# Values ahead of the first attention step, more staging tiles for the last tokens, earlier value transfers: one change to a two-branch attention kernel

## Chip, cores and metric

The kernel runs on one core of a Trainium2 chip. The metric is the device time of one execution in microseconds (us), lower is better. Every figure below is of executions in the undisturbed ("fast") state; the runs of one kernel lie within 0.1% to 0.7% of each other.

## The reference, cut to what matters

The result is a gated sum of two branches over the same 2048 x 576 input. Branch A is recurrent: 64 segments of 32 tokens, each with 8 memory tokens that the segment before it produced. Branch B is plain softmax attention with 32 heads of 18 columns.

```python
g = sigmoid((x * gate_w).sum(-1))
# A, 32 heads of 128:
for s in range(64):
    h = concat([mem, x[32*s : 32*s+32]])          # 8 + 32 tokens
    q, k, v = h @ Wq, h @ Wk, h @ Wv              # 576 -> 4096 each
    o = softmax(mask(q k^T * scale)) v @ Wo
    mem, out[s] = o[:8], o[8:]                    # mem goes to segment s + 1
# B, 32 heads of 18:
b = softmax(q k^T * scale) v @ wo                 # all 2048 tokens
return g * a + (1 - g) * b
```

Only the memory makes A serial. The q, k and v of tokens do not depend on it, so the kernel computes those of the **last 8 tokens** of each segment ahead of time, for 16 segments together. Branch B is cut into 512 **attention steps** (two groups of matmuls and one Exp of 128x2048 on ScalarE), which fill the gaps that A's chain leaves.

## The kernel before

It has three stages. The **prologue** transposes x, projects Q, K and V of branch B in blocks, stores them in DRAM in a layout by head, loads A's weights (14.2 MB), and does the first of four last-token stages (24 blocks). The **segments** run A, with B's steps and the other last-token stages in between. The **tail** folds the last segments' leftovers and projects the output of B in 16 row blocks.

```python
def load_weights(w, src):                       # six pieces each for wv, wq, wk
    for c in range(NF):
        yield nc.gpsimd.dma_start(out=w[0][:, c, :], in_=...)
    ...
def in_turn(dma):                               # a piece waits for the one before the last
    if len(ready) > 1: add_dependency(dma, ready[-2])
    ready.append(dma)

def last_tokens(q, share, k=None):
    store = nc.sync if share else nc.gpsimd
    xlb = fil.tile([P, NF + 2, P], BF16, name="xlb", bufs=1)
    nc.sync.dma_start(out=xlb..., in_=xld[q])   # the tokens of 16 segments
    for b in range(HD // 512):                  # 8 blocks of V
        ...matmuls into pv...
        vl = fil.tile([P, 512], BF16, name="vl")        # pool fil: two tiles
        copy_out(vl, pv, share); store.dma_start(out=vld[...], in_=vl)
    for w, dstd in ((wq, qld), (wk, kld)):      # 8 + 8 blocks of Q and K
        for b in range(H // 4):
            ...matmuls into pv...
            vl = fil.tile([P, 512], BF16, name="vl")
            copy_out(vl as (s h t), pv as (h s t), share)
            store.dma_start(out=dstd[q]...[:, :, 4*b*LO:4*(b+1)*LO], in_=vl)  # runs of 64 bytes

def project_vb(hf, kb, share):                  # one value block of B, one half of the heads
    vt = vts[kb % 4]                            # four tiles, zero-filled at the start
    ...matmuls into pv...
    copy_out(vt[:, :, 0:DhB], pv, share)
    nc.sync.dma_start(out=vgd[...], in_=vt)
...                                             # prologue: x, blocks 0, 4, 5, first half of the values
for blk in FIRST: store_qk(blk, (0,))
for w, src in ((wv, A_Wv), (wq, A_Wq), (wk, A_Wk)):
    for d in load_weights(w, src): in_turn(d)
...
load_first()                                    # first K, V and Q chunks of B
for blk in FIRST: store_qk(blk, range(1, GB))
for blk in (1, 6, 2, 7): ...project_qk, attention steps between, store_qk...
for kb in range(NKB): project_vb(1, kb, 0); between(0.7)
for blk in (3, 8): ...
```

The softmax here doesn't subtract the row's maximum and nothing guards it: scores larger than these inputs give would overflow.

## Time and profile before

| | before |
|---|---|
| median of the first three runs | 1713.55 us (1712.34 to 1716.27) |
| profiled run (span of the core) | 1708.60 us (1706.9) |
| TensorE, ScalarE, VectorE busy | 88%, 67%, 56% of the span |
| mean granted TensorE clock | 0.967 |
| attention steps done ahead of the segments | 35 of 512 |

In profile rows, PE is TensorE, PEld its weight loads, DVE VectorE, ACT ScalarE, POOL GpSimd and SP SyncE; L823 is a line of the kernel, and `a<-b` means that a is written from b. Of the tiles, kch, vch and qch are chunks of B's K, V and Q, stg stages a Q/K block on its way to DRAM (qtd, ktd), vt stages values of B (to vgd; the five new ones are called xn), vl stages last tokens (tm in the changed kernel's first stage; in the segments tm is a copy of A's new q, k or v), and v_sb holds the values of one segment of A.

The profile gives, for each engine, rows of work with the idle time ahead of them in brackets and what ended that idle time. TensorE is the busiest engine, so its brackets are where time can be had. The prediction shows the large ones. The waits of TensorE summed over the segments are a second view; its columns are engine and line, releaser, us in total, times, longest. First one line of segments 1 to 62, then one of the last-token stage ahead of the segments (155 to 240 us):

```profile
PE pso L823 <- DMA v_sb<-tm: 11.8, 11, 2.3
```

```profile
PE pv L319 <- DVE vl L293: 15.8, 13, 2.5
```

The reader sees two causes that the change addresses: value transfers inside the segments (v_sb<-tm), and staging tiles of the last tokens that are not free yet (vl: 13 waits, none long). A third, the load of the last tokens themselves (xlb), is among the prediction's rows.

### The profile page before, as it was taken

How to read it: one execution, taken by the hardware profiler on the slowest of the kernel's cores; microseconds unless marked ns; L12 is line 12 of the kernel's file. 1: busy time of each engine (PE TensorE's matmuls, PEld its weight loads, DVE VectorE, ACT ScalarE, POOL GpSimd, SP SyncE). 2: the span in 40 equal slices, each digit the busy share in tenths (PEclk: the TensorE clock that was granted, in tenths of full speed). 3: DMA queues.
4: the chain of work that ended last, by engine and by line, in shares of the span. 5: the costliest groups of instructions: out<-in, count | busy, mean ns of one | idle time of the engine just before them, and what ended most of it. 6: DMA issues, size and time to landing. Idle time of an engine off the chain costs nothing. (4 is left out here: it accounts for less than half of the span.)

```text
span 1706.9 us, 57602 instructions
## 1 busy us (share of the span) xinstructions
PE 1494.8 (88%) x25082; PEld 789.3 (46%) x25082; DVE 963.4 (56%) x2360; ACT 1138.6 (67%) x976; POOL 364.6 (21%) x716
## 2 busy tenths in 40 slices
PE   6476669989999899999999999999999989899986
PEld 3232434445555444454555444555554444444444
DVE  2133245666666566656666656666666656565654
ACT  2154335767777676766776767777777787887873
POOL 5211111122222112131313121322221212120221
PEclk9788879999999999999999999999999999999998
DMA  7875431212221111121212111121211111111133
GB/s 191 277 266 185 106 63 33 58 35 46 50 51 45 43 37 52 44 48 35 59 38 56 42 43 47 46 47 36 58 42 48 33 46 32 45 32 31 30 103 103
DMA packets 127464, 114.38 MB, mean 67 GB/s; under 512 B 62531, under 2 KB 115011, under 8 KB 125619
## 3 DMA queue, kind: packets, MB, share of 16 engines
q1 hardware_dynamic: 106395, 59.03, 13.0%
q0 software_dynamic: 19872, 49.38, 10.9%
q8 instruction: 196, 3.21, 0.8%
q10 hardware_dynamic: 944, 2.29, 0.4%
q14 instruction: 57, 0.47, 0.1%
HBM read 60.94 MB, written 36.10 MB: 57 GB/s over the span
## 5 line engine op out<-in xcount | busy, mean ns | idle before, releaser
L257 ACT ACTIVATE etb<-sb 128x2048 bf16<-128x2048 f32 x512 | 959.5, 1874 | 420.2 <-PE sb L238 420.2
L752 DVE CAST tm<-pvv 128x512 bf16<-128x512 f32 x384 | 264.1, 688 | 170.5 <-PE pvv L740 169.1
L740 PEld LDWEIGHTS <-ht 128*32 128x32 bf16 x7680 | 187.0, 97 | 184.3 <-DVE ht L876 12.6
L238 PE MATMUL sb<-qch,kch 32*128 32x512 bf16 x2048 | 204.8, 389 | 55.6 <-ACT etb L257 36.9
L222 PE MATMUL ob<-etb,vch 128*32 128x512 bf16 x2048 | 206.8, 394 | 5.4 <-DVE tq L159 5.1
L835 DVE CAST ot<-pso 128x320 bf16<-128x320 f32 x256 | 120.3, 487 | 124.3 <-PE pso L823 120.5
L629 PE MATMUL acc<-wo,ot 128*32 128x384 bf16 (+1 forms) x4096 | 158.9, 291 | 5.4 <-DVE ot L835 3.6
L740 PE MATMUL pvv<-wq_m,ht 128*32 128x512 bf16 x2048 | 135.9, 386 | 12.6 <-DVE ht L876 7.1
L740 PE MATMUL pvv<-wk_m,ht 128*32 128x512 bf16 x2048 | 134.4, 383 | 0.0
L740 PE MATMUL pvv<-wv_m,ht 128*32 128x512 bf16 x2048 | 134.1, 382 | 0.0
L238 PEld LDWEIGHTS <-kch 32*128 32x128 bf16 x2048 | 61.7, 91 | 146.5 <-issue 111.4
L685 POOL DMA_DIRECT2D a_dram<-rl x192 | 95.9, 534 | 140.3 <-DVE rl L681 136.5
L629 PEld LDWEIGHTS <-ot 128*32 128x32 bf16 x4096 | 104.6, 97 | 45.8 <-DVE ot L835 11.6
L842 POOL COPY otl<-ot 128x256 bf16<-128x256 bf16 x64 | 27.1, 424 | 392.6 <-DVE ot L835 358.9
L222 PEld LDWEIGHTS <-vch 128*32 128x32 bf16 x2048 | 52.7, 93 | 123.7 <-issue 117.3
L293 DVE CAST vl<-pv 128x512 bf16<-128x512 f32 x96 | 65.9, 686 | 73.7 <-DMA qld<-vl 18.6
L823 PE MATMUL pso<-et,v_sb 64*128 64x40 bf16 x2048 | 82.0, 179 | 22.7 <-DMA v_sb<-tm 11.8
L811 ACT ACTIVATE lt<-pss 128x320 f32<-128x320 f32 x128 | 55.9, 437 | 68.0 <-PE pss L807 58.0
L823 PEld LDWEIGHTS <-v_sb 64*128 64x128 bf16 x2048 | 62.9, 93 | 72.5 <-issue 49.0
L767 PE MATMUL pt<-ident,tm 128*128 128x128 bf16 x1024 | 95.7, 221 | 0.8 <-DVE tm L752 0.8
L640 DVE CAST hl<-acc 128x384 bf16<-128x384 f32 (+1 forms) x128 | 57.7, 451 | 56.2 <-PE acc L629 55.9
L775 DVE COPY kt<-pt 128x512 bf16<-128x512 bf16 x128 | 53.8, 420 | 63.0 <-PE pt L767 63.0
(136 smaller groups left out, 1886.9 us busy)
## 6 DMA issues: line engine op xcount, KB each, us to landing
v_sb<-tm SPq DMA_DIRECT2D x512, 32.0 KB
wo<-in_A_Wo_dram POOLq DMA_DIRECT2D x4, 1152.0 KB, 8.1
vgd<-vt SPq DMA_DIRECT2D x32, 128.0 KB
wv_m<-in_A_Wv_dram POOLq DMA_DIRECT2D x4, 1024.0 KB, 8.1
wq_m<-in_A_Wq_dram POOLq DMA_DIRECT2D x4, 1024.0 KB, 8.2
wk_m<-in_A_Wk_dram POOLq DMA_DIRECT2D x4, 1024.0 KB, 9.1
v_sb<-vld SPq DMA_DIRECT2D x128, 32.0 KB
xl<-qld SPq DMA_DIRECT2D x64, 64.0 KB
```

The costliest lines, as they stand in the source:

```text
L222: nc.tensor.matmul(ob[32 * j:32 * j + 32, :], lhsT=vc[:, o + 32 * j:o + 32 * j + 32], rhs=et4[:, j, :], start=(kb == 0), stop=(kb == NKB - 1),
L238: nc.tensor.matmul(sb[:, j, :], lhsT=kc[32 * j:32 * j + 32, o:o + P], rhs=qch[gq][32 * j:32 * j + 32, :], start=True, stop=True, tile_posi ...
L257: nc.scalar.activation(out=before[:, :, :], in_=sb[:, :, :], func=ACT.Exp, scale=scale_b)
L293: nc.vector.tensor_copy(out=out, in_=in_)
L629: nc.tensor.matmul(acc[32 * j:32 * j + 32, 0:d1 - d0], lhsT=o[:, h, 0:CT], rhs=wo[:, h, d0:d1], start=(b == 0 and i == 0), stop=(b == 1 an ...
L640: nc.vector.tensor_copy(out=hl[:, 0, d0:d1], in_=acc[:, 0:d1 - d0])
L685: nc.gpsimd.dma_start(out=rows4[m, seg - LO:seg, i * n:(i + 1) * n], in_=rl[32 * i + m * LO:32 * i + (m + 1) * LO, :],)
L740: nc.tensor.matmul(pv[32 * j:32 * j + 32, :], lhsT=ht[:, cc, :], rhs=rw, start=(c == 0), stop=(c == NF), tile_position=(0, 32 * j),)
L752: nc.vector.tensor_copy(out=sbt[x][:, :], in_=ps[x][:, :])
L767: nc.tensor.transpose(out=pt[:, which, :, :, :].rearrange("p j (u i) t -> p j u i t", i=4)[:, :, :, i, :], in_=sbt[x][:, i * Dh:(i + 1) * Dh],
L823: nc.tensor.matmul(pso[:, i * L:(i + 1) * L], lhsT=v_sb[64 * jj:64 * jj + 64, b * 1024 + i * Dh:b * 1024 + (i + 1) * Dh], rhs=et[64 * jj:6 ...
L835: nc.vector.tensor_copy(out=ot[:, j * HG:(j + 1) * HG, :].rearrange("p h t -> p (h t)"), in_=ps["o", b, jj][:, 0:W8],)
```

## The change

Its intent is to take waits for transfers off TensorE's path at both edges and in the segments:

- The first K, V and Q chunks of B are loaded ahead of A's weights; the weights wait for them.
- All second-half values are projected ahead of every other block and step, into nine tiles instead of four; the five new ones lie on the tiles of x and are zero-filled on GpSimd.
- The first last-token stage gets four staging tiles instead of two. Its rows go to DRAM as whole kilobytes, and the 64-byte runs are on the side that reads them in the segments. Twelve of 14 copies of zero rows (the "pads") move from the prologue into the first segments.
- xlb is loaded one stage ahead; the q and k of the last tokens one segment ahead.
- The value transfer of a segment (`v0`, `v1` in its order) is issued right at its copy (`cV0`, `cV1`).
- In the tail, the leftovers go ahead of all but the first of the 16 row blocks, part of their stores goes to SyncE, and B's last divisions move.

```diff
+    load_first()
+    ready.extend([first_loads[-1]] * 2)
+    for d in pieces:                                  # A's weights
+        in_turn(d)
...
-    for blk in (1, 6, 2, 7):  ...project_qk, between, store_qk...
+    for i in range(5):
+        vt = pw.tile([P, Dm], BF16, name="xn", bufs=5)[:, 0:HV * 32]...
+        nc.gpsimd.memset(vt, 0.0)
+        nc.gpsimd.memset(vt[:, :, DhB:DhB + 1], 1.0)
+        vts.append(vt)
     for kb in range(NKB):
-        project_vb(1, kb, 0)
-        between(0.7)
-    for blk in (3, 8):
+        project_vb(1, kb, 3)
+    for blk in (1, 6, 2, 7, 3, 8):
...
+        stage = (lambda: seg2.tile([P, 512], BF16, name="tm", bufs=4)) if share else (
+            lambda: fil.tile([P, 512], BF16, name="vl"))
-        xlb = fil.tile([P, NF + 2, P], BF16, name="xlb", bufs=1)
-        nc.sync.dma_start(out=xlb..., in_=xld[q])
+        xlb = xlbs.pop(q)                             # load_xlb(q + 1) at the stage's end
-                store.dma_start(out=dstd[q]...[:, :, 4 * b * LO:4 * (b + 1) * LO], in_=vl)
+                store.dma_start(out=dstd[q, b], in_=vl[:, :])
...
-   ... V0 cK1 B E : pk0 Q1 S0 cV0 cQ1 x0 ... / S1 m0 v0 B F1 ... : v1 B l1 ...
+   ... V0 cK1 B E : pk0 Q1 S0 cV0 v0 cQ1 x0 ... V1 pq1 p0 cV1 v1 l0 r0 / S1 m0 B F1 ...
...                                                   # tail
-    for m in range(n):  finish(m), with a leftover after m = 2 to 10
+    group_rows(0, n_seg - 1)(); g0(); g1(); finish(0); group_last(2, n_seg - 1)()
+    for n in range(1, 6): finish(n)
+    while late: late_part()
+    load_rows(NT - 1)
+    for n in range(6, NT): finish(n)
```

More of the change, by code (lines that the diff above doesn't have):

```diff
@@ L88 @@
     xld = dpool.tile([n_seg // SG, P, (NF + 2) * P], BF16, name="xld")
-    qld = dpool.tile([n_seg // SG, P, SG * H * LO], BF16, name="qld")
-    kld = dpool.tile([n_seg // SG, P, SG * H * LO], BF16, name="kld")
+    qld = dpool.tile([n_seg // SG, H // 4, P, SG * 4 * LO], BF16, name="qld")
+    kld = dpool.tile([n_seg // SG, H // 4, P, SG * 4 * LO], BF16, name="kld")
     aw1 = ctx.enter_context(tc.tile_pool(name="aw1", bufs=1))
@@ L197, in load_kv @@
             vch[g, kc] = bint.tile([P, KC * P], BF16, name="vch", bufs=6)
-            loads.dma_start(
+            first_loads[:] = [loads.dma_start(
                 out=vch[g, kc][:, :].rearrange("p (k f) -> p k f", f=P),
                 in_=vgd[kc * KC:(kc + 1) * KC, :, g * P:(g + 1) * P].rearrange("k p f -> p k f"),
-            )
+            )]
         def load_q(i):
@@ L260, in b_steps @@
         late.extend(divisions(ob, GB * NQC - 1))
-        while late:
-            late_part()
-    loads = nc.sync
+    loads, first_loads = nc.sync, []
     bgen = b_steps()
@@ L293, in copy_out, with load_xlb @@
             nc.vector.tensor_copy(out=out, in_=in_)
+    xlbs = {}
+    def load_xlb(q):
+        if q < n_seg // SG:
+            xlbs[q] = fil.tile([P, NF + 2, P], BF16, name="xlb", bufs=1)
+            nc.sync.dma_start(out=xlbs[q][:, :, :].rearrange("p c t -> p (c t)"), in_=xld[q])
     def last_tokens(q, share, k=None):
         k = k or [None]
+        stage = (lambda: seg2.tile([P, 512], BF16, name="tm", bufs=4)) if share else (
+            lambda: fil.tile([P, 512], BF16, name="vl")
+        )
         store = nc.sync if share else nc.gpsimd
-        xlb = fil.tile([P, NF + 2, P], BF16, name="xlb", bufs=1)
-        nc.sync.dma_start(out=xlb[:, :, :].rearrange("p c t -> p (c t)"), in_=xld[q])
+        xlb = xlbs.pop(q)
         for b in range(HD // 512):
@@ L306, in last_tokens @@
                 nc.tensor.matmul(pv[:, :], lhsT=xlb[:, cc, :], rhs=rw, start=(c == 0), stop=(c == NF))
-            vl = fil.tile([P, 512], BF16, name="vl")
+            vl = stage()
             yield
@@ L321, in last_tokens @@
                         )
-                vl = fil.tile([P, 512], BF16, name="vl")
+                vl = stage()
                 yield
@@ L328, in last_tokens @@
                 )
-                store.dma_start(
-                    out=dstd[q].rearrange("p (s f) -> p s f", s=SG)[:, :, 4 * b * LO:4 * (b + 1) * LO],
-                    in_=vl[:, :].rearrange("p (s f) -> p s f", s=SG),
-                )
+                store.dma_start(out=dstd[q, b], in_=vl[:, :])
+                if w is wk and b == H // 4 - 1:
+                    load_xlb(q + 1)
                 yield
@@ L384 @@
     for i in range(4):
-        vt = pp.tile([P, HV, 32], BF16, name=f"vt{i}")
-        nc.gpsimd.memset(vt[:], 0.0)
+        vt = pp.tile([P, HV, 32], BF16, name=f"vt{i}")[:, :, :]
+        nc.gpsimd.memset(vt, 0.0)
         nc.gpsimd.memset(vt[:, :, DhB:DhB + 1], 1.0)
@@ L438, in project_vb @@
     def project_vb(hf, kb, share):
-        vt = vts[kb % 4]
+        vt = vts[(kb + 4 * hf) % len(vts)]
         pv = bank(None, [P, QC], FP32, "pvb")
@@ L451, in project_vb @@
         nc.sync.dma_start(
-            out=vgd[kb, :, hf * HV * 32:(hf + 1) * HV * 32], in_=vt[:, :, :].rearrange("p h e -> p (h e)")
+            out=vgd[kb, :, hf * HV * 32:(hf + 1) * HV * 32], in_=vt.rearrange("p h e -> p (h e)")
         )
     FIRST = (0, 4, 5)
+    pieces = [(w, src) for w, src in ((wv, A_Wv), (wq, A_Wq), (wk, A_Wk))]
+    pieces = (d for w, src in pieces for d in load_weights(w, src))
     for t in range(NQC):
@@ L463 @@
         )
+        if t == 0:
+            load_xlb(0)
         for blk in FIRST:
             project_qk(blk, t, 2)
+        if t == NQC - 1:
+            for blk in FIRST:
+                store_qk(blk, (0,))
         for kb in range(4 * t, 4 * t + 4):
             project_vb(0, kb, 2)
-    for blk in FIRST:
-        store_qk(blk, (0,))
-    for w, src in ((wv, A_Wv), (wq, A_Wq), (wk, A_Wk)):
-        for d in load_weights(w, src):
-            in_turn(d)
+    load_first()
+    ready.extend([first_loads[-1]] * 2)
+    for d in pieces:
+        in_turn(d)
     pgs = ps_bo.tile([P, NT], FP32, name="pgs", tag="ob")
@@ L499, in between @@
             b_advance(1)
-    load_first()
     for blk in FIRST:
         store_qk(blk, range(1, GB))
-    for blk in (1, 6, 2, 7):
-        for t in range(NQC):
-            project_qk(blk, t, 0)
-            between(1.1)
-        store_qk(blk, range(GB))
+    for i in range(5):
+        vt = pw.tile([P, Dm], BF16, name="xn", bufs=5)[:, 0:HV * 32].rearrange("p (h e) -> p h e", e=32)
+        nc.gpsimd.memset(vt, 0.0)
+        nc.gpsimd.memset(vt[:, :, DhB:DhB + 1], 1.0)
+        vts.append(vt)
     for kb in range(NKB):
-        project_vb(1, kb, 0)
-        between(0.7)
-    for blk in (3, 8):
+        project_vb(1, kb, 3)
+    for blk in (1, 6, 2, 7, 3, 8):
         for t in range(NQC):
@@ L527, with pad @@
         )
-    for g in range(1, GB):
+    fix = actx.enter_context(tc.tile_pool(name="fix", bufs=1))
+    seg2 = actx.enter_context(tc.tile_pool(name="seg2", bufs=2))
+    def pad(g):
         for t in (qtd, ktd):
-            in_turn(nc.gpsimd.dma_start(out=pads(t, g), in_=pads(t, 0)))
+            nc.gpsimd.dma_start(out=pads(t, g), in_=pads(t, 0))
+    pad(1)
     for i, _ in enumerate(last_tokens(0, 1 << 30)):
@@ L545 @@
     later = later_tokens()
-    fix = actx.enter_context(tc.tile_pool(name="fix", bufs=1))
-    seg2 = actx.enter_context(tc.tile_pool(name="seg2", bufs=2))
     cap = const.tile([P, L], BF16, name="cap")
@@ L684, in rest @@
                 for m in range(4):
-                    nc.gpsimd.dma_start(
+                    eng = nc.sync if s3 == n_seg - 1 and m % 2 else nc.gpsimd
+                    eng.dma_start(
                         out=rows4[m, seg - LO:seg, i * n:(i + 1) * n],
@@ L931 @@
         7: """
-        Q0 cQ0 K0 B E : cK0 / K1 tq0 tk0 pq0 V0 cK1 B E : pk0 Q1 S0 cV0 cQ1 x0 tk1 n0 B E : tq1 pk1 V1
-        pq1 p0 cV1 l0 r0 / S1 m0 v0 B F1 w00 x1 n1 o00 F2 cF1 p1 w01 E : v1 B l1 cF2 o01 r1 m1 E : F0
+        Q0 cQ0 K0 B E : cK0 / K1 tq0 tk0 pq0 V0 cK1 B E : pk0 Q1 S0 cV0 v0 cQ1 x0 tk1 n0 B E : tq1 pk1
+        V1 pq1 p0 cV1 v1 l0 r0 / S1 m0 B F1 w00 x1 n1 o00 F2 cF1 p1 w01 E : B l1 cF2 o01 r1 m1 E : F0
         a00 w10 cF0 w11 B E : o10 o11 ol a01 a10 a11 B / E : h0 g0 h1 g1 f0 ht0 f1 ht1 og oh
@@ L936 @@
         8: """
-        Q0 B E : V0 cQ0 K0 cV0 B / cK0 E : tq0 pq0 Q1 tk0 pk0 cQ1 B / E : S0 K1 tq1 x0 cK1 B n0 v0 tk1 E
-        : V1 pk1 pq1 p0 cV1 S1 l0 r0 x1 / B E : F0 m0 n1 v1 w00 o00 F1 cF0 p1 w01 o01 cF1 l1 r1 m1 B F2
+        Q0 B E : V0 cQ0 K0 cV0 v0 B / cK0 E : tq0 pq0 Q1 tk0 pk0 cQ1 B / E : S0 K1 tq1 x0 cK1 B n0 tk1 E
+        : V1 pk1 pq1 p0 cV1 v1 S1 l0 r0 x1 / B E : F0 m0 n1 w00 o00 F1 cF0 p1 w01 o01 cF1 l1 r1 m1 B F2
         a00 cF2 w10 o10 w11 E : B E : o11 ol a01 a10 h0 a11 g0 B h1 g1 f0 E : f1 ht0 ht1 oh og
@@ L974, in load_last @@
     def load_last():
+        while late:
+            late_part()
         nc.vector.memset(wol, 0.0)
@@ L1012, in finish, with load_qk @@
         nc.sync.dma_start(out=out_td[n * P:(n + 1) * P, :], in_=ofin[n])
+    xls = []
+    def load_qk(s):
+        sq, si = divmod(s, SG)
+        w = 4 * LO
+        for srcd in (qld, kld):
+            xl = seg2.tile([P, H, LO], BF16, name="xl")
+            nc.sync.dma_start(
+                out=xl[:, :, :].rearrange("p (b h) t -> p b (h t)", h=4),
+                in_=srcd[sq, :, :, si * w:(si + 1) * w].rearrange("b p f -> p b f"),
+            )
+            xls.append(xl)
+    load_qk(0)
     for s in range(n_seg):
@@ L1016 @@
             put_x(s + 1)
-        sq, si = divmod(s, SG)
+        if 2 + s < GB:
+            pad(2 + s)
         for jj in range(2):
@@ L1023 @@
             )
-        for dst, srcd in ((qt, qld), (kt3, kld)):
-            xl = seg2.tile([P, H, LO], BF16, name="xl")
-            nc.sync.dma_start(
-                out=xl[:, :, :].rearrange("p h t -> p (h t)"), in_=srcd[sq, :, si * H * LO:(si + 1) * H * LO]
-            )
-            nc.gpsimd.tensor_copy(out=dst[:, :, CT:L], in_=xl[:, :, :])
+        for dst in (qt, kt3):
+            nc.gpsimd.tensor_copy(out=dst[:, :, CT:L], in_=xls.pop(0)[:, :, :])
         width = 8 if s >= n_seg - eights else 7
@@ L1042 @@
                 f(*args)
+            if name == "S1" and s + 1 < n_seg:
+                load_qk(s + 1)
             if s == n_seg - 1 and name == LOAD_LAST:
@@ L1045 @@
         assert not todo
-    n = NT - 1
-    for m in range(n):
-        finish(m)
-        if m == 2:
-            r = group_rows(None, n_seg - 1)
-        if m == 3:
-            r()
-        if m in (4, 6):
-            r = group_span(None, m // 2 - 2)
-        if m in (5, 7):
-            r()
-        if m == 9:
-            r = group_last(None, n_seg - 1)
-        if m == 10:
-            r()
-            load_rows(n)
-    finish(n)
+    turns[0] = 0
+    g0 = group_span(1, 0)
+    g1 = group_span(2, 1)
+    group_rows(0, n_seg - 1)()
+    g0()
+    g1()
+    finish(0)
+    group_last(2, n_seg - 1)()
+    for n in range(1, 6):
+        finish(n)
+    while late:
+        late_part()
+    load_rows(NT - 1)
+    for n in range(6, NT):
+        finish(n)
     actx.close()
```

## The prediction

> **What bounds the kernel now.** I read the page first (engines, the 40 slices, groups), then the busy table by stretches, then TensorE's timeline with what ended each of its idle times. TensorE is 88% busy, and the slices show three stages: a prologue to 234.6 us that alternates between work and idling, 64 recurrent segments to about 1656 us, and a tail of 50 us. The stretch table, in us: TensorE, weight loads, VectorE, ScalarE, GpSimd busy, then granted clock, DMA share and GB/s:
>
> ```profile
> 58.70:74.60 15.90, 0.03 (x1) 0.00 (x0) 0.00 (x0) 0.00 (x0) 2.10 (x4) 0.66 0.96 321
> 159.46:228.50 69.04, 47.98 (x480) 30.96 (x480) 18.09 (x30) 26.51 (x15) 8.00 (x15) 0.83 0.54 126
> 262.30:1656.40 1394.10, 1297.67 (x23355) 681.75 (x23351) 863.30 (x2157) 1027.60 (x849) 301.97 (x597) 0.99 0.18 44
> 1662.60:1706.90 44.30, 28.50 (x239) 18.55 (x239) 18.98 (x40) 15.21 (x32) 6.50 (x13) 0.85 0.33 107
> ```
>
> In the segments TensorE is busy 93%, so little is to be had there. The edges are loose: 21 us idle of 69 while the first last tokens are projected, 16 of 44 in the tail. TensorE's timeline names what ended the large idle times (start, length, work, idle before, releaser):
>
> ```profile
> 74.67 0.61 PE L238 MATMUL sb<-qch,kch 32*128 32x512 bf16 x4 [15.94 <-DMA kch<-ktd]
> 83.36 2.29 PE L416 MATMUL pq<-xT,wb 128*128 128x512 bf16 x5 [5.83 <-DVE stg L293]
> 122.40 2.56 PE L443 MATMUL pvb<-wb,xT 128*128 128x288 bf16 x10 [8.50 <-DVE vt L293]
> 159.46 1.89 PE L306 MATMUL pv<-wv_m,xlb 128*128 128x512 bf16 x4 [13.48 <-DMA xlb<-xld]
> 233.71 0.24 PE L602 MATMUL ptm<-ident,m 8*128 8x8 bf16 x4 [5.23 <-DMA vch<-vgd]
> ```
>
> All of these are transfers, or buffers that a transfer holds. A further wait of 6.25 us for xlb<-xld lies inside segment 0 (254.47 us). GpSimd's timeline shows why transfers are slow here: the weights of 14.2 MB are issued from it one by one, two in flight.
>
> ```profile
> 53.70 1.19 POOL L106 DMA_DIRECT2D wv_m<-in_A_Wv_dram  x2
> 61.55 0.53 POOL L106 DMA_DIRECT2D wv_m<-in_A_Wv_dram  x1 [6.66 <-DMA wv_m<-in_A_Wv_dram]
> ...
> 121.63 0.51 POOL L108 DMA_DIRECT2D wk_t<-in_A_Wk_dram  x1 [3.94 <-DMA wk_m<-in_A_Wk_dram]
> ```
>
> The bracket is the point: GpSimd stands still until an earlier piece has landed. In the tail, TensorE idles behind the leftovers of the last segment, and the last row block waits for a store and a load of them:
>
> ```profile
> 1662.62 0.29 PE L864 MATMUL pw<-sel,hl 128*128 128x32 bf16 x4 [3.32 <-DVE hl L643]
> 1679.47 1.41 PE L994 MATMUL po<-wq_m 128*128 128x288 bf16 x10 [2.18 <-DVE hll L643]
> ...
> 1684.86 4.29 PE L994 MATMUL po<-wq_m 128*128 128x288 bf16 x20 [1.86 <-DVE hll L643]
> ```
>
> The chain of waits ends the same way: the load of a_dram, 2.27 us from 1700.54, then the last VectorE work at 1702.90.
>
> **What the Trainium skill says.** "DMA: Bandwidth & Descriptors", section "Anatomy of one DMA — SWDGE (gpsimd) path": a semaphore wait of a DMA happens on the sequencer that issues it, before dispatch. The trace agrees (6.66 us of GpSimd standing before the third piece), and this decides my prediction. The same page, "Rules for kernel authors": a strided last dimension costs one descriptor per contiguous run. The trace agrees: from GpSimd, 128 KB land in 2.2 us for vld<-vl (1 KB runs) but in 4.5 and 4.9 us for qld and kld (runs of 64 bytes). "TensorE: Matmul & The Clock Gate", Part 1: after about 3.4 us of idling the array falls to half rate. The trace agrees: five matmuls of pq took 2.29 us after the 5.83 us idle, and 1.25 us at 103.18 us.
>
> **The change part by part.** I compared the instruction orders of both built kernels.
>
> *Head loads ahead of the weights.* The first K, V and Q chunks are issued before the weights, which wait for the last of them. But xlb now stands on the SyncE queue from the first round and waits there for its xld store, some 4 us ahead of x loads; I allow 1.5 us. Projections then end near 56, stores and loads land near 66 (nine stores, four stores and nine loads at about 0.45 us each from 53.5, plus 2 to 3 us), so the weights start near 66 instead of 53.7.
>
> *All values first.* The 16 value projections of the second half stand before every attention step, so the early K brings nothing by itself. They use five new tiles, cleared on GpSimd, and in the built order those ten fills stand behind the last weight piece. GpSimd blocks on each piece, so the first value can only be copied out when that piece is issued. The traffic then is 14.2 MB and about 1 MB of stores, at 300 to 321 GB/s (the stretch table) 47 to 51 us, less about 3 for the final pieces: near 113 us. TensorE idles from about 58 to 113, where it did 14 Q/K blocks and 8 attention steps before. The values then take 16 x 0.65 = 11 us, to 124.
>
> *24 Q/K blocks.* Before, five blocks with three attention steps took 8.3 us (91.32 to 99.60), 1.66 per block with the link busy: 24 x 1.66 = 40, to 164. The waits of 5.83 and 8.50 do not return, the weights being in.
>
> *Last tokens, first 24 blocks.* xlb is there already, but the first staging tile lies over released memory and waits for the last K stores: 5 us. Before, 69 us for 24 blocks, 2.9 each, held by two tiles and slow stores. With four tiles, 1 KB rows and 12 of 14 padding copies moved into the segments, I take the engine work: 1.2 us of matmuls with 0.61 attention steps of 1.87 us of Exp; alternating one and two blocks per step gives 1.75. 24 x 1.75 = 42, to 211. Five us to load mem0 (6.0 before): segment 0 starts near 216 to 217 instead of 234.6. **Gain 17.5.**
>
> *Segment 0.* xlb is loaded ahead: **gain 6.**
>
> *Value transfers at their copy.* In the segments TensorE waited 11.8 us for v_sb<-tm. I take **9**. The 64-byte runs are now on the reading side (xl<-qld, xl<-kld), issued a segment ahead, and the link is 18% busy: nothing.
>
> *Attention steps moved.* 29 instead of 35 steps precede the segments, so six more segments carry eight steps instead of seven. Segments 8 to 35 took 22.31 us on average, 36 to 47 with eight steps 22.18: nearly free, **loss 1.**
>
> *Tail.* The last divisions leave the path of the final fold (3.32 us idle, gain 2.5). The leftovers go ahead of the 16 row blocks, and half of their stores to SyncE. The work is then 3 us of leftovers and 16 blocks; the last four took 1.24 us each without waits, I take 1.35: 21.6. From 1660.3 that is 1685, a little more for start and VectorE's late divisions 1688, and 3.1 us after VectorE as before: 1691 against 1706.9. **Gain 15.5.**
>
> Sum: 17.5 + 6 + 9 - 1 + 15.5 = 47, so 1713.5 - 47 = 1667 us.
>
> **Rivals.** *The five tiles' fills hold everything* longer: if the weights come at the old pace (68 us from first to last issue), the first value is copied at 134 and the prologue gains nothing (-3): 1687. For it: two pieces in flight took 8 us each. Against: the link then also carried some 7 MB of other traffic. *The prologue's DMA was only idling in disguise*: the weights are needed at 159 anyway, and TensorE still has 70 us of projections and attention after them, so ScalarE's Exp chain (2.4 us per step at best) may set 24 + 24 blocks rather than stores; then last tokens stay near 2.2 us each, 1678. For it: before, the best steps there came every 2.4 to 2.9 us. *The tail becomes bound by the loads* of otd through SyncE (1659 to 1671 us), and gains 8: 1675. *Reading in 64-byte runs slows v_sb*: 128 loads that take twice as long, ring-ordered after the value transfers, which speaks against more than 5 us.
>
> **Range and chances.** The prologue is uncertain by 12 us either way (weights' rate, hand-over), the tail by 5, the segments by 6; together about 14. So 1667 us, from 1648 to 1688. Two per cent is 1679.3; that is 12 us off, so chances are 0.78 faster, 0.20 within, 0.02 slower.
>
> **What would show it right or wrong.** In the changed profile: TensorE idle from about 58 us until close after the last weight issue (110 to 120), its releaser VectorE's copies into xn and theirs GpSimd's fills; no waits for vgd<-vt or stg; 24 last-token blocks in 40 to 48 us; segment 0 from 212 to 222; v_sb waits under 3 us; the last fold without its 3.32 us; the tail near 35 us after the last segment. It is wrong if fills run before the weights (then 1640 or less), if last tokens keep waiting for stores, or if segments lengthen by over 0.3 us each.

## The result, and the profile after

The median is 1667.93 us (1666.59 to 1668.76, 4 runs) against 1714.07 us (1712.34 to 1716.27, 4 runs) of the kernel before. A ratio is the mean time of one kernel's fast runs over that of the other's of the same rounds, so not quite the ratio of the medians: here 0.9729, with a 95% interval of 0.9713 to 0.9746. The changed kernel is faster, by 46 us.

The two profiled spans differ by less, 1706.9 - 1664.9 = 42.0 us, because the profiled run of before (1708.60) was faster than its four other runs. They are split here at the first Q projection of segment 0, the copy of a segment's last-token outputs in segments 0 and 62, and the end:

| part | before | after | gained | predicted |
|---|---|---|---|---|
| up to segment 0 | 234.6 | 226.3 | 8.3 | 17.5 |
| segment 0 | 27.7 | 20.0 | 7.7 | 6 |
| segments 1 to 62 | 1373.0 | 1358.9 | 14.1 | 8 (9 - 1) |
| segment 63 and tail | 71.6 | 59.7 | 11.9 | 15.5 |
| sum | 1706.9 | 1664.9 | 42.0 | 47 |

The total came out as predicted; its parts did not, and their errors partly cancel. TensorE's timeline of the changed kernel, with the rows that answer to those of before:

```profile
120.86 11.03 PE L449 MATMUL pvb<-wb,xT 128*128 128x288 bf16 x65 [59.74 <-DVE xn L291]
...
183.25 1.86 PE L313 MATMUL pv<-wv_m,xlb 128*128 128x512 bf16 x4 [7.53 <-DVE tm L291]
...
225.27 0.24 PE L616 MATMUL ptm<-ident,m 8*128 8x8 bf16 x4 [3.35 <-DMA xg<-xtd]
```

The waits for kch, stg, vt and xlb of the prologue are gone, and one wait of 59.74 us stands in their place: the first second-half value cannot be copied out of its bank. GpSimd's timeline says why:

```profile
68.64 1.10 POOL L106 DMA_DIRECT2D wv_m<-in_A_Wv_dram  x2 [12.13 <-DMA qtd<-stg]
...
119.26 0.52 POOL L108 DMA_DIRECT2D wk_t<-in_A_Wk_dram  x1 [2.66 <-DMA wk_m<-in_A_Wk_dram]
119.77 0.54 POOL L518 MEMSET xn<- 128x512 bf16 x1
```

The fills of the new tiles are issued by the engine that issues the weights, after them, and each weight piece waits there for an earlier one. A fill of half a microsecond begins 51 us after the first weight piece. The Trainium skill, "PSUM — Partial Sum Buffer", section "Engine vs sequencer instructions", says that GpSimd's queue is a strict FIFO; these rows agree.

The second view, VectorE's waits around the first staging tile of the last tokens (171 to 190 us), shows what the 7.53 us are: the new tiles lie in memory that the prologue's tiles had, and their K stores have not landed.

```profile
DVE tm L291 <- DMA ktd<-stg: 10.7, 1, 10.7
```

In segments 1 to 62, TensorE's wait for the value transfers fell from 11.8 us to:

```profile
PE pso L838 <- DMA v_sb<-tm: 2.0, 3, 1.1
```

The rows of the two window tables for segments 1 to 62, first of before, then of after (columns as in the prediction), show equal work and less idling of TensorE, 94.4 us against 79.5:

```profile
262.30:1635.30 1373.00, 1278.58 (x23015) 672.14 (x23011) 851.15 (x2127) 1010.45 (x835) 292.77 (x578) 0.99 0.18 43
```

```profile
246.30:1605.20 1358.90, 1279.37 (x23053) 670.62 (x23045) 852.22 (x2132) 1020.73 (x841) 265.79 (x588) 0.99 0.20 46
```

Of the 14.9 us less idling, 9.8 are v_sb and 0.9 xlb; the rest is spread over other rows. In the tail of the changed kernel, the last fold waits hardly at all, and the row blocks run almost without a break:

```profile
1632.31 0.26 PE L879 MATMUL pw<-sel,hl 128*128 128x32 bf16 x4 [0.15 <-DVE hl L657]
...
1639.61 8.33 PE L1011 MATMUL po<-wq_m 128*128 128x288 bf16 x65 [1.10 <-DVE rl L695]
```

The 150 matmuls of the last 15 row blocks, which begin with this row, have one more break, of 1.70 us. From the last segment's output copy (1656.4 before, 1628.7 after) to the end it takes 36.2 us instead of 50.5. Segment 63 itself became 2.5 us longer: TensorE waits there for v_sb<-tm four times (0.46, 0.22, 1.15 and 0.26 us), where the kernel before shows no such wait. That the earlier issue of these transfers does this is not shown: with the late transfers of e3 segment 63 took 22.8 us against 23.5 here and 21.1 before, with two such waits (0.59 and 1.05 us), and with the old tail of e4 23.4 us.

### The profile page after: what moved, and what is told of

Its sections match the earlier page's. It is cut to its first block, busy times and chain, and to the rows that moved or that the text cites. A ratio compares the mean times of both kernels' runs of the same rounds, so it can differ in the third digit from the quotient of the medians.

```text
span 1664.9 us, 57761 instructions
## 1 busy us (share of the span) xinstructions
PE 1476.0 (89%) x25082; PEld 781.3 (47%) x25082; DVE 960.2 (58%) x2355; ACT 1140.1 (68%) x981; POOL 335.8 (20%) x725
## 2 busy tenths in 40 slices
DMA packets 210089, 114.39 MB, mean 69 GB/s; under 512 B 159715, under 2 KB 197475, under 8 KB 208243
## 3 DMA queue, kind: packets, MB, share of 16 engines
q1 hardware_dynamic: 188971, 58.40, 15.8%
## 4 chain that ended last, share of the span: by engine, by line
PE 69%; ACT 11%; DVE 11%; DMA 5%; issue 2%; POOL 1%; SPq 1%; ACTq 0%; DVEq 0%; POOLq 0%
PE pvv L755 26%; ACT etb L257 8%; PE sb L238 8%; PE ob L222 7%; PE pt L782 5%; PE pv L326 4%; PE psh L800 3%; PE acc L643 3%; PE pso L838 2%; PE pq L422 2%; PE pv L313 2%; DVE hl L657 2%; DVE ot L850 2%; DVE hl L654 2%; ACT rq L830 2%
## 5 line engine op out<-in xcount | busy, mean ns | idle before, releaser
L755 PEld LDWEIGHTS <-ht 128*32 128x32 bf16 x7680 | 185.6, 96 | 183.6 <-DVE ht L891 14.1
L838 PE MATMUL pso<-et,v_sb 64*128 64x40 bf16 x2048 | 81.4, 178 | 14.3 <-DVE hll L657 5.3
L782 PEld LDWEIGHTS <-tm 128*128 128x128 bf16 x1024 | 57.8, 98 | 67.0 <-issue 49.4
```

The source lines that it names most:

```text
L755: nc.tensor.matmul(pv[32 * j:32 * j + 32, :], lhsT=ht[:, cc, :], rhs=rw, start=(c == 0), stop=(c == NF), tile_position=(0, 32 * j),)
L782: nc.tensor.transpose(out=pt[:, which, :, :, :].rearrange("p j (u i) t -> p j u i t", i=4)[:, :, :, i, :], in_=sbt[x][:, i * Dh:(i + 1) * Dh],
L838: nc.tensor.matmul(pso[:, i * L:(i + 1) * L], lhsT=v_sb[64 * jj:64 * jj + 64, b * 1024 + i * Dh:b * 1024 + (i + 1) * Dh], rhs=et[64 * jj:6 ...
```

## The experiments

Each experiment alters the changed kernel unless another base is named. They ran in batches, each batch on a chip of its own beside the kernel before, so kernels of different batches are compared by their ratio to before. One hundredth of that ratio is 17 us. All results were correct.

| run | edit | median us | ratio to before (95%) | against the changed kernel |
|---|---|---|---|---|
| (changed kernel) | | 1667.93 | 0.9729 (0.9713 to 0.9746) | |
| e1_fills_first | fills ahead of the weights | 1628.11 | 0.9501 (0.9466 to 0.9536) | -39 |
| e2_weights_first | weights ahead of B's first loads | 1663.75 | 0.9711 (0.9674 to 0.9748) | -3 |
| e3_v_late | old place of the value transfers | 1683.99 | 0.9820 (0.9776 to 0.9863) | +16 |
| e4_tail_old | old tail | 1685.82 | 0.9842 (0.9809 to 0.9875) | +19 |
| e5_two_tiles | two staging tiles | 1679.58 | 0.9795 (0.9776 to 0.9815) | +11 |
| e6_old_layout | 64-byte stores | 1673.75 | 0.9762 (0.9743 to 0.9781) | +6 |
| e7_values_between | old order of the values | 1637.13 | 0.9553 (0.9526 to 0.9580) | -30 |
| e8_stores_after | e1, and 15 stores later | 1624.28 | 0.9474 (0.9454 to 0.9493) | -44 |
| e9_stage_old | old staging in full | 1699.35 | 0.9911 (0.9895 to 0.9927) | +31 |
| e10_xlb_late | xlb loaded at its stage | 1702.86 | 0.9920 (0.9899 to 0.9942) | +33 |
| e11_wo_gated | e8, and wo held back | 1621.59 | 0.9457 (0.9441 to 0.9473) | -47 |
| e12_first_two_vl | e11, first two blocks elsewhere | 1622.41 | 0.9469 (0.9451 to 0.9487) | -45 |

The last column is the difference of the ratios times 1714 us.

### Is it the fills that hold TensorE for 60 us?

The theory is that the position of the ten fills on GpSimd sets the first copy. The rival is that the link, full of weights, sets it. The first run moves the fills and nothing else:

```diff
     load_first()
     ready.extend([first_loads[-1]] * 2)
+    for i in range(5): ...two fills each, vts.append(vt)
     for d in pieces:
         in_turn(d)
...
-    for i in range(5): ...two fills each, vts.append(vt)
```

> The changed kernel (1668 us) with one move: the ten fills of the five new value tiles are issued on GpSimd before the weights' transfers instead of after them. My theory: TensorE's 59.7 us idle before the values is GpSimd standing behind the weight pieces; then the values run at about 60 to 85 us beside the weights, the 24 Q/K blocks end near 130 instead of 172, segment 0 starts near 180 to 190 instead of 226, and the time falls by 35 to 45 us to 1623 to 1633. Rival: the weights' own arrival (last piece issued at 119, landed at about 122) sets the prologue, or their traffic slows the 16 stores and the Q/K stores so much that the idle time only moves to them; then the time falls by under 12 us.

It took 1628.11 us (1622.30 to 1629.75), 39 us less. GpSimd's and TensorE's timelines of this kernel:

```profile
58.63 0.17 POOL L485 MEMSET xn<- 128x16 bf16 x1
67.48 1.10 POOL L106 DMA_DIRECT2D wv_m<-in_A_Wv_dram  x2 [8.68 <-DMA vch<-vgd]
```

```profile
80.12 2.56 PE L449 MATMUL pvb<-wb,xT 128*128 128x288 bf16 x10 [14.60 <-DVE xn L291]
```

The fills run in time in which GpSimd stood still anyway. The 59.74 us shrink to 14.60 us, and 1.24 us more a little later, and now it is VectorE waiting for value stores (15.43 us for vgd<-xn). So the theory holds, and 15 us of the rival's cause are real.

The second run asks whether loading B's first chunks ahead of the weights is worth it:

```diff
-    load_first()
-    ready.extend([first_loads[-1]] * 2)
     for d in pieces:
         in_turn(d)
+    load_first()
```

> The changed kernel with the weights issued ahead of the first K, Q and V chunks again, as before the change. My theory: since the attention steps stand behind the values and the values behind the last weight piece, the early chunks buy nothing and only delay the weights; first weight piece at about 56 instead of 68.6 us, last at about 108 to 112 instead of 119, values 8 to 11 us earlier, time 6 to 11 us lower than the changed kernel (1657 to 1662). Rival: the chunks ahead are what removed the 15.94 us wait for K; then putting the weights first costs 10 us or more (1678 or above).

It took 1663.75 us: the direction is as expected, the size is smaller, and the intervals overlap. The weights start at 56.48 instead of 68.64 us, but take 61 us from first to last issue instead of 50.6, and TensorE still idles 58.05 us. Of the 12 us of an earlier start, 10 are given back. The likely cause is that the stores and loads that stood ahead of the weights now share the link: it moved 282 GB/s between the first and the last issue here, 288 in the changed kernel, so that the rate is much the same and the bytes are more.

### Is it worth having all values ahead?

This run undoes that part, with its tiles and fills: the values come back between the Q/K blocks and steps.

```diff
-    for i in range(5): ...fills...
+    for blk in (1, 6, 2, 7): ...project_qk, between, store_qk...
     for kb in range(NKB):
-        project_vb(1, kb, 3)
-    for blk in (1, 6, 2, 7, 3, 8):
+        project_vb(1, kb, 0)
+        between(0.7)
+    for blk in (3, 8):
```

> The changed kernel with the second half of the values back between the Q/K blocks, on the old four tiles, so without the new tiles and their fills. My theory: the values ahead of all attention, as built, stop TensorE for 59.7 us; without them the Q/K blocks and attention steps run beside the weights from 60 us on, and segment 0 starts near 190 to 198 instead of 226: 1632 to 1642, 26 to 36 us faster than the changed kernel. Rival: the order of the values is worth something in itself and the old order brings its waits back (5.8 for staging, 8.5 for value tiles) and more; then 1655 or above.

It took 1637.13 us (1632.15 to 1642.98), 30 us less than the changed kernel, as expected. So this part, as built, loses 30 us of what the others gain. The idea is not wrong: with the fills in front (0.9501 against 0.9553 here) it is some 9 us better than the old order (two batches, and the intervals just touch), where 2.19 us for kch, 3.27 for stg and 9.43 for the value tiles came back.

### What holds TensorE after that?

In e1 the values wait for their own stores, which stand on SyncE's queue behind 15 stores of Q and K blocks. This run has e1's fills and sends those 15 stores after the values:

```diff
+    for kb in range(NKB):
+        project_vb(1, kb, 3)
     for blk in FIRST:
         store_qk(blk, range(1, GB))
-    for kb in range(NKB):
-        project_vb(1, kb, 3)
```

> The kernel with early fills (1628 us) and the 15 stores of the first Q/K blocks moved behind the value stores on the SyncE queue. My theory: its 14.6 us wait at 80 us comes from value stores standing behind those 15 stores and the weights; with this the values end near 70 instead of 86, at the price of 2 to 6 us for a staging tile: 1614 to 1621. Rival: the stores are slow because the weights fill the link, not because of their place; then within 4 us of 1628.

It took 1624.28 us, 4 us less than e1 (5 by the ratios) with overlapping intervals, so the time is what the rival said, and not 1614 to 1621. The wait moved: the values wait 2.79 us, and the next Q/K block waits for its staging tile, whose store is now later.

```profile
68.28 4.22 PE L449 MATMUL pvb<-wb,xT 128*128 128x288 bf16 x20 [2.79 <-DVE xn L291]
...
86.46 2.29 PE L422 MATMUL pq<-xT,wb 128*128 128x512 bf16 x5 [10.29 <-DVE stg L291]
```

Together 13.1 us where e1 has 15.8. In e1 the link was already moving 280 GB/s from 62 to 80 us; with the stores in another order the same bytes have to leave. That the link is the bound is argued from this figure; no run lightened it.

### Staging of the last tokens

Three runs split this part. Two tiles instead of four:

```diff
-        stage = (lambda: seg2.tile([P, 512], BF16, name="tm", bufs=4)) if share else (
-            lambda: fil.tile([P, 512], BF16, name="vl"))
+        stage = lambda: fil.tile([P, 512], BF16, name="vl")
```

> The changed kernel with the first 24 last-token blocks staged again in the two small tiles of before; the layout in whole kilobytes is kept. My theory: with 1 KB rows a store lands in a bit over 2 us, so two tiles give one block per copy 0.69 + issue 0.4 + landing 2.2, halved: about the 1.75 us that the engines need; only under the output weights' traffic does the second pair matter (5 to 10 us lost), and the 7.5 us wait of the first tile for the last K stores falls away. Within 6 us of the changed kernel (1662 to 1674). Rival: the tiles are what shortened this stage from 69 to about 50 us; then 10 us or more is lost (1678 or above).

It took 1679.58 us, 11 us more, so my theory fell and the rival was right. TensorE's waits in this stage (165 to 240 us) and VectorE's:

```profile
PE ob L222 <- DVE tq L159: 7.1, 1, 7.1
PE pv L311 <- DVE vl L291: 6.0, 1, 6.0
```

```profile
DVE vl L291 <- DMA vld<-vl: 18.9, 4, 9.9
```

The second TensorE wait is not a staging wait by name, but it is one by cause: VectorE stands at a vl copy until a store lands (9.9 us at the longest) and does the division of B's step (tq) late. Old layout with four tiles:

```diff
-    qld = dpool.tile([n_seg // SG, H // 4, P, SG * 4 * LO], BF16, name="qld")
+    qld = dpool.tile([n_seg // SG, P, SG * H * LO], BF16, name="qld")
...
-                store.dma_start(out=dstd[q, b], in_=vl[:, :])
+                store.dma_start(out=dstd[q]...[:, :, 4 * b * LO:4 * (b + 1) * LO], in_=vl...)
```

> The changed kernel with the old layout of the last tokens' queries and keys (stores in runs of 64 bytes, loads in runs of 512), four tiles kept. My theory: a store then lands in 4.5 to 5 us instead of about 2, which four tiles cover (4 x 1.75 = 7 us), and loads get cheaper; between 2 us faster and 6 us slower than the changed kernel (1666 to 1674). Rival: the layout is what shortened the stage, since small runs load the link and the SyncE queue; then 10 us or more slower (1678 or above).

It took 1673.75 us, 6 us more, at the upper end of my range; the rival is not borne out. The third run puts all of the old staging back: two tiles, old layout, and all pads in the prologue.

> The changed kernel with the whole last-token staging of before: two staging tiles, rows stored as 64-byte runs on the writing side, all padding copies in the prologue. My theory: the three parts add up, two tiles about +12 us and the old layout about +6 us as measured alone, so 1686 to 1693 us. Rival: they overlap, because with two tiles the stage waits for the stores anyway: at most +14 us, under 1682 us.

It took 1699.35 us, 31 us more, above both expectations: two tiles and the old layout alone give only 11 + 6 = 17. TensorE's waits from 165 to 260 us:

```profile
PE pv L324 <- DVE vl L291: 14.0, 10, 2.7
PE ptm L618 <- DMA m<-in_A_mem_dram: 7.6, 1, 7.6
```

Two further waits are of 5.9 us (vl) and 5.0 us (tq). The ten waits of L324 (the Q and K blocks) are in neither e5 nor e6, and TensorE waits 4.3 us longer for segment 0's first loads (7.6 against 3.35). The pads were not put back alone, so whether the remaining 14 us are theirs or come of slow stores meeting two tiles stays open.

### xlb one stage ahead

```diff
     def last_tokens(q, share, k=None):
+        load_xlb(q)
...
-                if w is wk and b == H // 4 - 1:
-                    load_xlb(q + 1)
```

> The changed kernel with the last-token values (xlb) loaded at the start of each last-token stage, as before, and not one stage ahead. My theory: segment 0 of the kernel before was some 6 to 8 us longer because of this load and the first staging wait of 7.5 us would hide a part of it here, so +8 to +16 us in all, 1676 to 1684 us. Rival: the load is hidden behind the wait for the first staging tile: under +4 us, below 1672 us.

It took 1702.86 us; five of six runs were within 0.8 us of that and one was 1693.17. That is 33 us more, twice the upper end of my expectation. TensorE waits 13.42 us for xlb in the first stage, where the changed kernel waits 7.53 for its first tile, and from 230 us on:

```profile
PE pv L314 <- DMA xlb<-xld: 18.8, 3, 7.7
```

The kernel before waited 7.1 us in the same three places. The load now stands on SyncE behind the eight early value transfers of a segment (7.11 us to issue) and the two loads of the next segment. The rest is a lower clock. The window table around the fourth stage, which starts near 954 us after a wait of 5.26 us:

```profile
954.00:958.00 4.00, 3.81 (x22) 1.28 (x22) 0.81 (x2) 1.10 (x3) 0.00 (x0) 0.50 0.00 0
```

The same view over segments 1 to 63:

```profile
260.00:1666.00 1406.00, 1311.95 (x23411) 684.01 (x23411) 863.57 (x2163) 1038.72 (x856) 274.54 (x607) 0.98 0.20 46
```

This stretch takes 1382.4 us in the changed kernel, 1299.38 of them busy. So here TensorE idles 11.0 us more (13.0 for the two later loads, less elsewhere) and is busy 12.6 us longer with the same matmuls: 23.6 us. Ahead of it 13.7 us are lost, of which 5.9 in the first stage and 5.9 in segment 0 are this load, and 1.1 us come back in the tail: 36.2 of the 36.3 us between the spans. Not all slower matmuls are explained, though: cut into pieces of 25 us, ten have a clock below 1.00 (five in the changed kernel), and only two of the ten hold one of these waits. Why the others do, and the one quicker run, stays open.

### Value transfers at their copy

```diff
-   ... cV0 v0 cQ1 ... cV1 v1 l0 r0 / S1 m0 B F1 ...
+   ... cV0 cQ1 ... cV1 l0 r0 / S1 m0 v0 B F1 ... : v1 B l1 ...
```

> The changed kernel with the value transfers back at their old, later places in both segment orders, everything else kept. My theory: the wait of TensorE for v_sb<-tm over the segments, 11.8 us before and 2.0 after, is what this part is worth: it comes back to 10 to 20 us (the loads of last tokens now stand ahead of some value transfers on the same queue), and the time rises by 8 to 18 us, to 1676 to 1686. Rival: the segments' gain of 14 us came from the staging, the layout or the loads issued a segment ahead; then this costs under 4 us.

It took 1683.99 us (1676.95 to 1687.98), 16 us more, as expected, but not by the waits alone. The profiled run is the slowest of the four. The window row of segments 5 to 28 of this kernel and TensorE's wait in them, then the same two views of the same segments of the changed kernel:

```profile
337.00:881.00 544.00, 503.96 (x9024) 269.10 (x9014) 334.54 (x831) 372.87 (x313) 106.77 (x237) 0.97 0.20 45
```

```profile
PE pso L838 <- DMA v_sb<-tm: 10.6, 6, 3.3
```

```profile
333.00:858.00 525.00, 493.80 (x9034) 266.39 (x9026) 333.85 (x830) 373.49 (x314) 107.85 (x237) 1.00 0.20 47
```

```profile
PE pso L838 <- DMA v_sb<-tm: 0.6, 1, 0.6
```

The stretch is 19 us longer: 10.0 us more waits for v_sb and 10.2 us of slower matmuls, nearly the same number, less 1.2 us of other idling. Three waits of 3.34, 3.26 and 2.98 us are most of it, and after the first and the last of them the granted clock was 0.50 for about 4 us (422 to 426 and 785.3 to 789.3 us). The two do not go together everywhere: the kernel before had 8.6 us of these waits in the same segments (eight, none over 2.34 us), but its matmuls took only about 1 us longer than the changed kernel's, and the stretch 532.8 us. The longer waits of e3 have a source that the kernel before lacks: the loads of q and k one segment ahead now stand ahead of the late value transfers on SyncE, which stood still 45.0 us at these loads (14 waits, up to 9.4 us; none in the changed kernel). So the two moves belong together, and neither's worth can be read from undoing one.

### The tail

```diff
-    group_rows(0, n_seg - 1)(); g0(); g1(); finish(0); ...
+    for m in range(n):  finish(m), with a leftover after m = 2 to 10    # as before
```

> The changed kernel with the old tail: leftovers of the last segments between the row blocks, their stores from GpSimd alone, the last divisions inside the attention steps. My theory: the tail is worth 12 to 15 us by itself (after the last segment 50.5 us before, 36.2 after), so 1680 to 1684, with the wait of about 4 us for the last a_dram load back. Rival: the tail shrank because less other traffic was left, not by its order; then under 5 us.

It took 1685.82 us, 19 us more, where I had expected 12 to 15. The last segment's output copy is at 1628.28 us, where it is at 1628.7 in the changed kernel; all of the difference lies after it, and the waits of before are back, such as the one of the fold (3.32 us then):

```profile
1635.17 0.29 PE L881 MATMUL pw<-sel,hl 128*128 128x32 bf16 x4 [3.43 <-DVE hl L659]
```

That tail takes 55.6 us from there, 5 more than in the kernel before; this was not followed up.

### The first staging tile's wait

In e8 the largest wait left in the last-token stage was 6.4 us for the first staging tile. Two runs look for its cause. The first holds back the output weights (wo, 4.7 MB) until the last K store, with e8 as its base:

```diff
-                nc.sync.dma_start(out=(qtd, ktd)[which]..., in_=...)
+                stores.append(nc.sync.dma_start(out=(qtd, ktd)[which]..., in_=...))
...
+    ready.extend([stores[-1]] * 2)          # ahead of the loads of wo
```

> The fastest kernel so far (fills first, first-block stores behind the value stores, 1624 us) with the output projection's weights held back until the last K store. My theory: those weights share the link with the first staging stores; without them the first tile's wait of 6.4 us falls to 2 to 4 us, 1618 to 1622 us. Rival: the stores are held by their own write path, no change within 2 us, 1622 to 1626 us.

It took 1621.59 us, 3 us less by the ratios, with overlapping intervals. The time lies in my range, but not for my reason: the wait did not fall (7.7 us), and VectorE still waits 10.8 us for ktd<-stg ahead of the first tile. So the traffic of wo is not what delays those stores. The second run, based on e11, stages the first two blocks in the two old tiles, whose memory is their own:

```diff
+        made = [0]
+        def stage():
+            made[0] += 1
+            if share and made[0] > 2:
+                return seg2.tile([P, 512], BF16, name="tm", bufs=4)
+            return fil.tile([P, 512], BF16, name="vl")
```

> The kernel with the output weights held back (1622 us, ratio to before 0.9457), and its first two last-token blocks staged in the two tiles that the later stages use, which stand in memory of their own; the four new tiles stand where the first stage's tiles stood, and VectorE waited 10.8 us for the last K stores before it wrote the first of them. My theory: that wait, not a lack of tiles, is the 7.7 us of TensorE in this stage; two blocks (2 x 1.75 us) can now run ahead of it, so the wait falls by 2 to 4 us, 1618 to 1620 us. Rival: the queue of stores is the bound and the wait comes back two blocks later in full: within 1.5 us, ratio above 0.945.

It took 1622.41 us, no change. TensorE's waits from 118 to 183 us:

```profile
PE pv L331 <- DVE tm L291: 5.9, 2, 4.0
...
PE pv L318 <- DVE tm L291: 1.8, 1, 1.8
```

The 7.7 us at the first tile became 1.8 us there and 5.9 us later. The rival is right: a free place for two more blocks does not help where the next ones wait for stores again. That SyncE's one queue of stores is the bound here is argued from these two runs, not shown by itself. e8, e11 and e12 are the fastest versions and equal within what was measured, some 44 to 47 us faster than the changed kernel.

## Why the prediction was right or wrong

The time was right: 1667 predicted, 1667.93 measured. By its own steps:

- **Head loads ahead of the weights.** The weights were put near 66 us and started at 68.64. That the early K brings nothing by itself was said; e2 shows that this order costs some 3 us, or nothing.
- **All values first.** The mechanism was right in every step: fills behind the last weight piece, TensorE idle from 58 us, released by VectorE's copies into xn. The size was off: the first value was put at 113 us and came at 120.9. Of these 7.9 us, 2.6 are the later start, 3.6 the pace (50.6 us from first to last issue where 47 were taken; the link moved 288 GB/s between them, not 300 to 321) and 1.6 the fill and copy after it. The values took 10.9 us (11 predicted). The prediction did not price this part alone: it costs 30 us as built (e7), and gains 9 with the fills in front (e1 against e7).
- **24 Q/K blocks**: 39.2 us, 40 predicted. (The count of what TensorE did before from 58 to 113 us, 14 blocks and 8 steps, holds up to 106 us only; values and steps followed. It does not enter the sum.)
- **Last tokens.** 51.0 us where 47 were predicted: the first tile waited 7.5 us, not 5, and the rest took 43.5, not 42. e5, e6 and e9 (11, 6 and 31 us slower) fit a stage that stores held. Two of the stated signs failed here: segment 0 began at 226.3 us, not between 212 and 222, and with the wait of the first tile the 24 blocks lie outside 40 to 48 us.
- The hand-over took 4.4 us, 5 predicted. So the **prologue's gain of 17.5** is the term that was mis-sized: it measured 8.3, by the late first value and the staging wait.
- **Segment 0**: 7.7 us, 6 predicted. e10 shows that loading xlb a stage ahead does far more than this, 33 us: without it the two later stages wait 13.0 us, where the kernel before waited 0.9, and the clock falls. The prediction priced only the wait in segment 0. That the early value transfers make the late load so dear is argued from SyncE's order: only the kernel before has both late, and it differs in much else.
- **Value transfers**: the wait fell by 9.8 us, 9 predicted, and segments 1 to 62 gained 14.1. The prediction's loss of 1 us for six more attention steps cannot be seen. The surplus of some 4 us over its terms is idle time of other rows and was not traced to a cause.
- **Tail**: 36.2 us after the last segment (near 35 predicted), and the fold's wait fell from 3.32 to 0.15 us. The gain of 11.9 instead of 15.5 comes mainly from segment 63, 2.5 us longer, which was not foreseen and whose cause stays open (see the profile after).

Of the **rivals**, the first came about in part: the fills held TensorE until 121 us, between the 113 of the prediction and the 134 of the rival. ScalarE's Exp did not set the last-token stage: 24 blocks in 43.5 us are 1.8 each, where that rival had near 2.2 (with the wait of the first tile they are 2.1, but that is a wait for stores). The loads of the tail did not bound it (14.3 us gained after the last segment, where that rival had 8), and 64-byte reads did no visible harm: packets under 512 bytes rose from 62,531 to 159,715 and the v_sb waits fell.

So the prologue was predicted 9 us too well and the tail 4, the segments 6 too badly and segment 0 by 2. That leaves 42 of 47 us between the profiles; between the medians it is 46, as the profiled run of before was quicker than its four other runs. The sum was closer than its parts deserve: that 1667 met 1667.93 is luck. What the prediction missed as a whole is interaction. Undone one at a time, the tail, the value transfers, the staging and xlb are worth 19 + 16 + 31 + 33 = 99 us, the values -30 and the head loads -3: 66 us, where the change gained 46.

## What to carry to other kernels

A fill or copy that is issued on an engine behind throttled transfers starts when the last of them is issued; put it ahead of them, or on another engine, and read the order on each engine before adding buffers. When a wait for a store is taken away, look where the next instruction that needs the same queue or link stands: in the changed kernel, in e8 and in e12 it only moved. A change of many parts can win while one of its parts loses; undo each part alone, and expect that the numbers will not add up.

## What the Trainium skill lacked or had wrong

- "DMA: Bandwidth & Descriptors", section "Anatomy of one DMA — SWDGE (gpsimd) path", has the wait on the issuing sequencer, and "PSUM — Partial Sum Buffer" has the FIFO queue. No page puts them together into the rule that other work on GpSimd stands behind its throttled transfers: here the first fill, of 0.54 us, began 51 us after the first weight piece, TensorE idled 59.74 us, and moving them was worth 39 us (e1).
- "DMA: Bandwidth & Descriptors", section "Bandwidth", gives 6.15 us for 1 MB. With two pieces of 1 MB in flight and small stores beside them, the pieces took a median of 5.4 to 7.6 us from issue to landing, and the link moved 288 GB/s in the changed kernel and up to 321 before; the page has no figure for such a mix, and the prediction's pace was 3.6 us too quick for it.
- "TensorE: Matmul & The Clock Gate", Part 1, names half rate after idling, which the clock of 0.50 after 5.26 us agrees with. The runs add to it: in the segments a shorter wait was followed by half rate too, 0.50 after 2.98 us (e3). There 10.0 us more of waits came with 10.2 us of slower matmuls, and in e10 11.0 us of idling with 12.6 us; in the kernel before 8.6 us in waits of at most 2.34 us came with about 1 us. No run tests how the loss grows with the length of a single wait.
